# Attention with an exact row maximum: maxima turned and keys loaded earlier, output stores later, the sums copied by VectorE, some maxima sent from two queues

## The chip, the core and the metric

The kernel runs on one core of a Trainium2 chip. Five engines work side by side, each on its own list of instructions in order: TensorE (PE, with its weight loads as PEld), VectorE (DVE), ScalarE (ACT), GpSimd (POOL) and SyncE (SP), which here only issues transfers. They meet through semaphores. A transfer (DMA) is issued by SP, ACT or POOL and then moved by 16 DMA engines. The metric is the device time of one execution in microseconds (us); lower is better. A time is the median of several runs, and one further execution was profiled.

## The reference

One transformer block on 2048 tokens of width 640, all in float32:

```
h  = x + attention(layernorm(x), wqkv) @ wo        # 32 heads of width 20, softmax over 2048 keys
h2 = h + (silu(layernorm(h) @ w_gate) * (layernorm(h) @ w_up)) @ w_down     # inner width 1728
```

The softmax subtracts the maximum of each row of scores, so the kernel needs, for every head and query, the largest of 2048 scores before it can take the exponentials of that row.

## The kernel before

**Stages.** Up to about 319 us the kernel normalizes x and computes queries, keys and values, and also the first maxima. From 319 to 1440 us it does attention. After that come the output projection of the last tokens and the gated two-layer part, whose weights were prepared during attention.

**Units and steps.** Attention is cut into 32 units. Unit u = 4 g + c handles the four heads of group g (8 groups) and the 512 queries of chunk c (4 chunks). A unit has 16 steps, one for each tile of 128 keys (`kt`). What a step does on the engines is set by the string `WhSmsSHMs`, letter by letter:

- `S`, `s` (four in all): scores of 128 keys against 512 queries for one head (line L1328, into one of four PSUM banks named `ps_one`), then the exponential on ACT (L1334, into `probs`).
- `m`, `M`: one 128x512 product for the row maxima of a later unit (L272 into one of three banks named `ps_max`) and its reduction on DVE (L292). `h` and `H`: two half products into one bank and one reduction (L307). So DVE has three reductions in a step.
- `W`: the weighing (L1338) of values by the exponentials of two steps ago, into the bank `acc` of the unit. With the last tile of a unit, which falls into step 1 of the next one, `row_sums` copies `acc` to the SBUF tile `o` on ACT (L1348), and four transfers on SP bring the row sums out of it (L1351, `r<-o`). After `W` come the calls that fell due for this step (`later`) and one task of the weight preparation, which works on POOL and SP (L1146, L1147, L1178 to L1242; stores L1137; loads of raw weights L1166, L1220).

**The maxima of a later unit.** When the last product of unit v has been reduced, `max_all` reduces its partial maxima to a tile `neg` (L315, DVE). This happens in the last step of a unit (v with c = 1), at step 5 (v with c = 2 and c = 0) or step 11 (v with c = 3). The maxima must stand as two extra rows in the queries of v (`q_stk`) before the first score of v. There are two ways.

- With long lead (22 units): `max_parts` splits `neg` in two parts on POOL, `max_turn` transposes them on DVE four steps later (L331) and stores them to DRAM (L332, `m_d<-turned`), and `max_load` reads them into the query rows six steps later (L342, four transfers `q_stk<-m_d`).
- With short lead (10 units: the first two and all with c = 3): `max_finish`, two steps later, transposes on PE (L347, into a `ps_one` bank), splits on ACT (L89) and DVE (L90) into a tile `m2`, and writes the rows with four transfers on SP (L354, `q_stk<-m`).

**The sums of the unit before.** At the end of step 4 DVE takes reciprocals of the row sums (L1359), which waits for `r<-o`; SP stores them (L1361), and reads them back spread over 128 partitions (L1367, `rb<-r_d`), which waits for the store. At the end of step 9 POOL multiplies `o` by them (L1373), and at the end of step 11 SP issues four stores of `o` (L1376). In the last two units all this is earlier.

**Loads.** At the end of step 6 SP loads the queries of unit u + 3 (four transfers). The keys of the next group are loaded in the units with c = 1, at the end of steps 8, 10, 12 and 14 (`load_keys`, four transfers each), the values of the next group in the units with c = 2 at the same steps (one transfer each).

SP works through all of this in one line: an issue that waits for its data holds back every issue written behind it.

Of the kernel before, what the change touches and what calls it, by code (L numbers as in the profile page):

```python
# [13 lines left out]
AF = mybir.ActivationFunctionType  # L14
# [16 lines left out]
NG = H // G  # L31
# [13 lines left out]
def tile_block(ctx: ExitStack, tc: tile.TileContext, x, wqkv, wo, wg, wu, wd, out):  # L45
    nc = tc.nc
# [41 lines left out]
    def split(src, hi, lo, lo_engine=nc.vector):  # L88
        nc.scalar.activation(hi, src, AF.Copy)  # L89
        lo_engine.tensor_tensor(out=lo, in0=src, in1=hi.bitcast(F32), op=ALU.subtract)  # L90
# [221 lines left out]
    def max_all(u):  # L312

        ends[u] = stk.tile([P, G * TPC], F32, name="neg", tag="neg", bufs=2)
        nc.vector.tensor_reduce(  # L315
            ends[u], mxs[u].rearrange("p b h t k -> p (b h t) k"), axis=AX.X, op=ALU.max, negate=True
        )
# [10 lines left out]
    def max_turn(u):  # L328

        turned = stk.tile([P, 2 * G * TPC], F32, name="turned", bufs=2)  # L330
        nc.vector.transpose(turned, ends.pop(u).bitcast(F32).rearrange("p i n -> p (i n)"))  # L331
        nc.sync.dma_start(m_d[u % 2], turned)  # L332

    def max_load(u):

        n = 2 * TPC
        rows = m_d[u % 2].rearrange("(q i r) c -> i r q c", q=4, i=2)
        for b in range(2):
            for i in range(2):
                row = b * ROW + NPART + i  # L340
                dst = queries[u][row : row + 1].bitcast(F32).rearrange("r j c -> r (j c)")
                nc.sync.dma_start(dst, rows[i, b * n : (b + 1) * n])  # L342

    def max_finish(u):

        m = (ps_one if u else ps_max)()[: G * TPC, :P]
        nc.tensor.transpose(m, ends.pop(u), ident)  # L347
        parts = stk.tile([G * TPC, 2, P], F32R, name="m2", tag="m2", bufs=1)
        split(m, parts[:, 0], parts[:, 1], nc.vector)
        for b in range(2):  # L350
            for i in range(2):
                row = b * ROW + NPART + i
                first = b * 2 * TPC
                nc.sync.dma_start(  # L354
                    queries[u][row : row + 1].bitcast(F32).rearrange(
                        "r j (t p) -> r (j t) p", t=TPC
                    ),
                    parts[first : first + 2 * TPC, i, :].bitcast(F32),
                )
# [963 lines left out]
    def scores(u, kt, j, probs):  # L1323

        p, b = divmod(j, 2)
        rows = slice(b * ROW, b * ROW + NPART + 2)
        ps = ps_one()
        nc.tensor.matmul(  # L1328
            ps,
            keys[u // NC][rows, p, kt * P : (kt + 1) * P],  # L1330
            queries[u][rows, p, :],
            start=True, stop=True,
        )
        nc.scalar.activation(probs[p][:, b, :], ps, AF.Exp, scale=scale)  # L1334
# [10 lines left out]

    def row_sums(acc, *queues):
        o = pc.tile([P, CH], F32, name="o", bufs=2)
        nc.scalar.activation(o, acc, AF.Copy)  # L1348
        r = pc.tile([P, 16], F32, name="r")
        for j in range(G):  # L1350
            queues[j % len(queues)].dma_start(  # L1351
                r[32 * j : 32 * j + 32, :],
                o[32 * j + DH : 32 * j + DH + 1, :].rearrange("r (p f) -> r p f", p=32),
            )
        return o, r
# [24 lines left out]
    todo, tail, accs, later, full, now = [], [], {}, {}, [], [0]  # L1380
    left = {u: sum(2 for a in rest if a[0] == u) for u in range(1, NU)}

    whole, halves_of = [], []

    def counted(u, n):
        left[u] -= n
# [3 lines left out]
    def next_max(b):  # L1390
        if not whole and rest:
            a = rest.pop(0)
            whole.extend((*a, i) for i in (b, 1 - b))
        if whole:
            a = whole.pop(0)
            max_one(*a)
            counted(a[0], 1)

    def next_half(b):

        if not halves_of and rest:
            a = rest.pop(0)
            halves_of.extend((i, a, []) for i in range(2))
        if not halves_of:
            return
        i, a, banks = halves_of[0]
        if not banks:
            banks.append(ps_max())
            max_half(banks[0], i, *a, b)
        else:  # L1410
            nc.tensor.keepalive_nop([nc.tensor.lower_ap(banks[0])])
            max_half(banks[0], i, *a, b)
            max_halves(banks[0], i, *a)
            counted(a[0], 2 * i)
            halves_of.pop(0)
# [11 lines left out]
    preparing = prepare_weights()  # L1427
# [3 lines left out]
    for u in range(NU):  # L1431
        g, c = divmod(u, NC)
        if g == NG - 1 and c >= 2:
            _, first, ln, flips, _ = ahead
            extra = [*first, *ln, lambda: None, *flips]
        for kt in range(NT):
            now[0] = u * NT + kt
            probs = [pp.tile([P, 2, CH], F32, name="probs") for _ in range(2)]
            heads = [[0, 2], [1, 3]]
            for op in ORDER if rest or whole or halves_of else LAST_ORDER:  # L1440
                if op in "mM":
                    next_max(int(op == "M"))
                elif op in "hH":
                    next_half(int(op == "H"))
                elif op in "sS":
                    scores(u, kt, heads[op == "S"].pop(0), probs)
                else:
                    if len(todo) == 2:
                        weigh_next()
                    for f in later.pop(now[0], ()):  # L1450
                        f()
                    if extra:
                        extra.pop(0)()
                    if preparing and u and kt not in (3, 4):
                        preparing.pop(0)()
                    if now[0] == (NU - NC) * NT + 8:
                        unit_ring, last_ring = weight_rings()
                        unit_ring.fill()
                        last_ring.fill()
            todo.append((u, kt, probs))  # L1460
            for v in full:
                max_all(v)
                if v % NC == NC - 1 or v == 1:
                    later.setdefault(now[0] + 2, []).append(lambda v=v: max_finish(v))
                else:
                    max_parts(v)
                    later.setdefault(now[0] + 4, []).append(lambda v=v: max_turn(v))
                    later.setdefault(now[0] + 6, []).append(lambda v=v: max_load(v))
            full.clear()
            if kt == 6 and u + 3 < NU:  # L1470
                load_queries(u + 3)
            if kt == 10 and u == 0:
                fill_ones(k_stk[1])
            if kt >= 8 and kt % 2 == 0 and c == 1 and g + 1 < NG:
                load_keys(g + 1, slice((kt - 8) // 2 * CH, (kt - 6) // 2 * CH))
            if kt >= 8 and kt % 2 == 0 and c == 2 and g + 1 < NG:
                load_values(g + 1, (kt - 8) // 2 * TPC, (kt - 6) // 2 * TPC)

            sooner = u >= NU - 2
            if kt == (3 if sooner else 4) and tail:  # L1480
                reciprocals(u - 1, tail[0][2], nc.sync)
                rb = spread(u - 1, nc.sync)
            if kt == (6 if sooner else 9) and tail:
                store_o(u - 1, tail[0][1], rb, nc.gpsimd, None)
            if kt == (7 if sooner else 11) and tail:
                store_o(u - 1, tail.pop()[1], rb, None, nc.sync)
            if g == NG - 1 and c >= 1:
                at = 8 if sooner else NT - 4
                if kt == at:
                    ahead = projection(  # L1490
                        c - 1, ps_max if c < NC - 1 else (lambda: ps_b())
                    )
                if kt in (at, at + 1, 12 if sooner else 14):
                    ahead[0][min(kt - at, 2)]()
                    if kt == at + 1 and c < NC - 1:
                        ahead[4]()
            k = 2 * (u - NU + 8)
            if kt in (12, 13) and 0 <= k + kt - 12 < ND:
                if k + kt == 12:
                    assert not preparing  # L1500
                    wo_hi = pc.tile([P, ND, D], F32R, name="wo_hi", bufs=1)
                    wo_lo = pc.tile([P, ND, D], F32R, name="wo_lo", bufs=1)
                load_wo(k + kt - 12)
            if kt in (2, 3) and 0 <= k + kt - 4 < ND:
                split_wo(k + kt - 4)
# [4 lines left out]
    u, o, r = tail.pop()  # L1510
# [561 lines left out]
```

## Time and profile before

| what | value |
|---|---|
| time, median of 3 runs | 2011.97 us (2009.52 to 2014.36) |
| the profiled execution's own time | 2012.87 us |
| its span, first to last instruction | 2010.4 us |
| granted TensorE clock, mean | 0.999 |
| busy over the span | PE 99%, DVE 80%, ACT 72%, POOL 39% |
| from 319 to 1300 us of the span | 981.00 us: PE 975.77, ACT 965.69, DVE 888.61, POOL 310.81 busy |

A row of the timeline has the start in us from the span's start, the duration in us, the engine, the line, the operation, what it writes and reads, the shapes and a count of equal instructions in a row. In brackets stands how long the engine had been idle before it, and what ended the idle time. `SPq` and `POOLq` mark the issue of a transfer. A row of the transfers' view gives the line, the count, the size of one in KB and the median time from issue to landing, which is known for POOL's issues only. PE's ends are modelled, so its busy share is no measure of its pace; here the distance from one weighing (L1338) to the next is the length of a step.

### The profile page before, as it was taken

How to read it: one execution, taken by the hardware profiler on the slowest of the kernel's cores; microseconds unless marked ns; L12 is line 12 of the kernel's file. 1: busy time of each engine (PE TensorE's matmuls, PEld its weight loads, DVE VectorE, ACT ScalarE, POOL GpSimd, SP SyncE). 2: the span in 40 equal slices, each digit the busy share in tenths (PEclk: the TensorE clock that was granted, in tenths of full speed). 3: DMA queues.
4: the chain of work that ended last, by engine and by line, in shares of the span. 5: the costliest groups of instructions: out<-in, count | busy, mean ns of one | idle time of the engine just before them, and what ended most of it. 6: DMA issues, size and time to landing. Idle time of an engine off the chain costs nothing. (4 is left out here: it accounts for less than half of the span.)

```text
span 2010.4 us, 41923 instructions
## 1 busy us (share of the span) xinstructions
PE 1985.1 (99%) x14794; PEld 1268.7 (63%) x14794; DVE 1599.5 (80%) x2831; ACT 1440.1 (72%) x2827; POOL 789.4 (39%) x1182
## 2 busy tenths in 40 slices
PE   8999999999999999999999999999999999999998
PEld 6999995444444444444444444455598888888887
DVE  5687778899999899998999999975477666676667
ACT  4678778999999999999999999987633222212221
POOL 7464424343453443443400011011155544844465
PEclk9999999999999999999999999999999999999999
DMA  7887563443634544435412132222268655974642
GB/s 244 255 258 257 183 206 78 128 140 105 193 103 141 152 135 138 157 127 175 150 60 68 40 86 58 79 63 62 62 215 278 228 168 174 359 248 160 203 146 93
DMA packets 199350, 310.48 MB, mean 154 GB/s; under 512 B 53744, under 2 KB 87856, under 8 KB 198120
## 3 DMA queue, kind: packets, MB, share of 16 engines
q1 hardware_dynamic: 192552, 284.21, 44.0%
q0 software_dynamic: 6496, 23.60, 4.0%
q8 instruction: 120, 1.97, 0.4%
q14 instruction: 86, 0.70, 0.1%
q10 hardware_dynamic: 96, 0.00, 0.0%
HBM read 208.11 MB, written 99.19 MB: 153 GB/s over the span
## 5 line engine op out<-in xcount | busy, mean ns | idle before, releaser
L1334 ACT ACTIVATE probs<-ps_one 128x512 f32<-128x512 f32 x2048 | 1056.1, 612 | 46.7 <-PE ps_one L1328 37.2
L292 DVE TENSOR_REDUCE mx<-ps_max 128x1 f32<-128x512 f32 x980 | 671.8, 686 | 90.6 <-PE ps_max L272 88.0
L272 PEld LDWEIGHTS ps_max<-k_stk,q_stk 60*128 60x128 f32 x1964 | 294.2, 185 | 462.8 <-DVE mx L307 393.5
L1328 PE MATMUL ps_one<-q_stk,k_stk 62*128 62x512 f32 x2048 | 570.4, 427 | 2.7 <-DMA q_stk<-m 1.8
L272 PE MATMUL ps_max<-k_stk,q_stk 60*128 60x256 f32 (+1 forms) x1964 | 565.5, 376 | 2.5 <-DVE mx L292 1.2
L1338 PE MATMUL acc<-probs,v_stk 128*32 128x512 f32 x4096 | 546.1, 605 | 0.1
L307 DVE TENSOR_REDUCE mx<-ps_max 128x2 f32<-128x512 f32 x492 | 335.8, 683 | 0.4 <-PE ps_max L272 0.4
L1328 PEld LDWEIGHTS ps_one<-q_stk,k_stk 62*128 62x128 f32 x2048 | 304.9, 184 | 15.0 <-ACT probs L1334 11.3
L1750 DVE TENSOR_TENSOR tmp<-ps_a,tmp 128x512 f32<-128x512 f32 x208 | 141.3, 690 | 122.2 <-PE ps_a L1535 96.6
L262 DVE TENSOR_REDUCE mx<-ps_max 128x2 f32<-128x512 f32 x288 | 180.8, 685 | 63.7 <-PE ps_max L240 60.2
L252 ACT ACTIVATE ps_max<-ps_max 128x512 f32<-128x512 f32 x288 | 151.6, 583 | 42.9 <-PE ps_max L240 40.3
L1629 PE MATMUL ps_b<-halves,yp 128*128 128x320 f32 x1032 | 179.0, 308 | 1.5 <-DMA halves<-j_d 1.3
L1629 PEld LDWEIGHTS ps_b<-halves,yp 128*128 128x128 f32 x1032 | 165.2, 188 | 17.5 <-POOL yp L90 1.5
L1535 PE MATMUL ps_a<-t,units 128*128 128x512 f32 x624 | 162.5, 396 | 0.0
L1338 PEld LDWEIGHTS acc<-probs,v_stk 128*32 128x32 f32 x4096 | 80.7, 108 | 128.1 <-issue 119.9
L90 POOL TENSOR_TENSOR yp<-y,yp 128x256 fp32r<-128x256 f32 x96 | 60.2, 628 | 189.7 <-ACT yp L89 189.7
L1535 PE MATMUL ps_a<-z,units 128*128 128x512 f32 x516 | 133.8, 394 | 0.0
L1535 PEld LDWEIGHTS ps_a<-t,units 128*128 128x128 f32 x624 | 112.6, 188 | 18.5
L1373 POOL TENSOR_TENSOR o<-o,rb 128x512 f32<-128x512 f32 x31 | 39.8, 1284 | 194.2 <-DMA rb<-r_d 60.6
L1634 DVE TENSOR_TENSOR h<-ps_b,h 128x320 f32<-128x320 f32 x248 | 110.1, 482 | 6.8 <-PE ps_b L1629 5.4
L671 PE MATMUL ps_one<-z_hi,w_lo 64*128 64x512 f32 x380 | 113.4, 392 | 0.0
L671 PE MATMUL ps_one<-z_lo,w_hi 64*128 64x512 f32 x380 | 112.1, 392 | 0.0
(228 smaller groups left out, 2746.5 us busy)
## 6 DMA issues: line engine op xcount, KB each, us to landing
units<-w_d SPq DMA_DIRECT2D x186, 256.0 KB
w_d<-stage SPq DMA_DIRECT2D x106, 256.0 KB
halves<-j_d SPq DMA_DIRECT2D x70, 320.0 KB
j_d<-stage SPq DMA_DIRECT2D x42, 320.0 KB
k_stk<-k_d SPq DMA_DIRECT2D x64, 160.0 KB
q_stk<-q_d SPq DMA_DIRECT2D x64, 160.0 KB
raw<-k_d SPq DMA_DIRECT2D x62, 160.0 KB
raw<-q_d SPq DMA_DIRECT2D x54, 160.0 KB
```

The costliest lines, as they stand in the source:

```text
L252: nc.scalar.activation(ps, ps, AF.Relu)
L262: nc.vector.tensor_reduce(mx[:, b, :, t, kc], ps.rearrange("p (j n) -> p j n", j=2), axis=AX.X, op=ALU.max,)
L272: nc.tensor.matmul(ps, queries[u][rows, pair, t * P : (t + 1) * P], keys[u // NC][rows, pair, k0:k1], start=True, stop=True, skip_group_ch ...
L292: nc.vector.tensor_reduce(mx[:, b, pair, t, kc : kc + 1], ps, axis=AX.X, op=ALU.max)
L307: nc.vector.tensor_reduce(max_slots(u)[:, :, pair, t, slot], ps.rearrange("p (j n) -> p j n", j=2), axis=AX.X, op=ALU.max,)
L671: nc.tensor.matmul(ps, a[rows], b[rows], start=(i == n == 0), stop=(i == 1 and n == last), skip_group_check=True,)
L1328: nc.tensor.matmul(ps, keys[u // NC][rows, p, kt * P : (kt + 1) * P], queries[u][rows, p, :], start=True, stop=True,)
L1334: nc.scalar.activation(probs[p][:, b, :], ps, AF.Exp, scale=scale)
L1338: nc.tensor.matmul(acc[32 * j : 32 * j + 32, :], values[u // NC][:, kt, j * VW : j * VW + 32], probs[j // 2][:, j % 2, :], start=(kt == 0) ...
L1535: nc.tensor.matmul(ps.rearrange("p (t n) -> p t n", t=TPC), w[k][:, i], z[k][:, :, j], start=(first and m == 0), stop=(last and m == len(n ...
L1629: nc.tensor.matmul(ps, a, b, start=(n == 0), stop=(n == len(pairs) - 1))
L1750: add = lambda out, ps, x: nc.vector.tensor_tensor(out=out, in0=ps, in1=x, op=ALU.add)
```

## The change

- `max_finish` is called at the end of the step behind the one in which `max_all` stood, that is ahead of the `W` which it used to follow. In the step in which it is due, the task of weight preparation is left out and comes one later. Its two transfers for the second half of the rows are issued by POOL, the first two by SP as before.
- `max_turn` comes three steps behind `max_all` instead of four, `max_load` five instead of six.
- The keys of the next group are loaded in units with c = 0 (in the first group still c = 1).
- Reciprocals, their store and `rb` come at the end of step 5 instead of 4; the stores of `o` in units with c = 2 at the end of step 13 instead of 11 (the last two units keep their own steps).
- `row_sums` copies `acc` on DVE instead of ACT, also after the last unit.

```diff
-                nc.sync.dma_start(
+                (nc.gpsimd if b else nc.sync).dma_start(
                     queries[u][row : row + 1].bitcast(F32).rearrange(
...
     def row_sums(acc, *queues):
         o = pc.tile([P, CH], F32, name="o", bufs=2)
-        nc.scalar.activation(o, acc, AF.Copy)
+        nc.vector.tensor_copy(o, acc)
...
-                    if preparing and u and kt not in (3, 4):
+                    if preparing and u and kt not in (3, 4) and not behind_step:
                         preparing.pop(0)()
...
             todo.append((u, kt, probs))
+            while behind_step:
+                behind_step.pop(0)()
             for v in full:
                 max_all(v)
                 if v % NC == NC - 1 or v == 1:
-                    later.setdefault(now[0] + 2, []).append(lambda v=v: max_finish(v))
+                    behind_step.append(lambda v=v: max_finish(v))
                 else:
                     max_parts(v)
-                    later.setdefault(now[0] + 4, []).append(lambda v=v: max_turn(v))
-                    later.setdefault(now[0] + 6, []).append(lambda v=v: max_load(v))
+                    later.setdefault(now[0] + 3, []).append(lambda v=v: max_turn(v))
+                    later.setdefault(now[0] + 5, []).append(lambda v=v: max_load(v))
...
-            if kt >= 8 and kt % 2 == 0 and c == 1 and g + 1 < NG:
+            if kt >= 8 and kt % 2 == 0 and c == (0 if g else 1) and g + 1 < NG:
                 load_keys(g + 1, slice((kt - 8) // 2 * CH, (kt - 6) // 2 * CH))
...
-            if kt == (3 if sooner else 4) and tail:
+            if kt == (3 if sooner else 5) and tail:
                 reciprocals(u - 1, tail[0][2], nc.sync)
...
-            if kt == (7 if sooner else 11) and tail:
+            if kt == (7 if sooner else 13 if c == 2 else 11) and tail:
                 store_o(u - 1, tail.pop()[1], rb, None, nc.sync)
```

On PE, in unit 6, the transposition of `max_finish` for unit 7 stands behind the weighing of step 13 before the change:

```order
L272 MATMUL ps_max<-k_stk_125,q_stk 128x512
L1328 MATMUL ps_one<-q_stk,k_stk_5605 128x512
L1338 MATMUL acc<-probs,v_stk_5606 32x512 x4
L347 MATMUL ps_one<-ident,neg 16x128
L272 MATMUL ps_max<-k_stk_125,q_stk 128x256
```

and now ahead of it:

```order
L272 MATMUL ps_max<-k_stk_125,q_stk 128x512
L1328 MATMUL ps_one<-q_stk,k_stk_5605 128x512
L347 MATMUL ps_one<-ident,neg 16x128
L1338 MATMUL acc<-probs,v_stk_5606 32x512 x4
L272 MATMUL ps_max<-k_stk_125,q_stk 128x256
```

The one weighing and the one transposition have changed places; the scores and products around them stand as before.

On SP, in unit 9 (c = 1), from the store of the turned maxima of unit 10 to the stores of `o`, before:

```order
L332 DMA m_d_70<-turned 128x32
L176 DMA k_stk_5605<-k_d_64 40x2x512
L176 DMA k_stk_5605<-k_d_64 20x2x512
L176 DMA k_stk_5605<-k_d_64 40x2x512
L176 DMA k_stk_5605<-k_d_64 20x2x512
L342 DMA q_stk<-m_d_70 1x32x32 x4
L1376 DMA o_d<-o 20x512 x4
```

and now:

```order
L332 DMA m_d_70<-turned 128x32
L1137 DMA w_d_84<-stage 128x512 x2
L1166 DMA raw<-in_B_w_gate 128x5x128
L1166 DMA raw<-in_B_w_up 128x5x128
L342 DMA q_stk<-m_d_70 1x32x32 x4
L1376 DMA o_d<-o 20x512 x4
```

The key loads have left this unit, and the weight preparation stands a little later in the program than before, so that a load of raw weights now lies between.

On SP, in unit 10 (c = 2), around the rows of maxima for unit 11, before:

```order
L193 DMA v_stk_5606<-v_d 128x4x96 x2
L1376 DMA o_d<-o 20x512 x4
L1137 DMA w_d_86<-stage 128x512
L193 DMA v_stk_5606<-v_d 128x4x96
L354 DMA q_stk<-m_11431 1x8x128 x4
```

and now, where the other two transfers `q_stk<-m` are on POOL:

```order
L193 DMA v_stk_5606<-v_d 128x4x96 x2
L354 DMA q_stk<-m_11412 1x8x128 x2
L193 DMA v_stk_5606<-v_d 128x4x96
L1376 DMA o_d<-o 20x512 x4
L193 DMA v_stk_5606<-v_d 128x4x96
```

The stores of `o`, which wait for POOL's multiplication, have moved behind the rows of maxima.

On POOL the two transfers come directly behind the first sums of the weight preparation (L1178, L1179):

```order
L1373 TENSOR_TENSOR o<-o,rb 128x512
L1178 TENSOR_TENSOR sums<-raw 128x256
L1179 TENSOR_TENSOR sums<-sums,raw 128x256
L354 DMA q_stk<-m_11412 1x8x128 x2
L1182 TENSOR_TENSOR sums<-raw 128x256
```

The two transfers stand between those sums and the next ones. Before, in the same unit, POOL issued none of them and the multiplication stood behind the first sums:

```order
L1178 TENSOR_TENSOR sums<-raw 128x256
L1179 TENSOR_TENSOR sums<-sums,raw 128x256
L1373 TENSOR_TENSOR o<-o,rb 128x512
L1182 TENSOR_TENSOR sums<-raw 128x256
```

So the multiplication has moved ahead of the first sums.

On DVE, in unit 5, the copy of `o` now stands between the last reduction of one step and the first of the next:

```order
L307 TENSOR_REDUCE mx_7742<-ps_max 128x2
L292 TENSOR_REDUCE mx_7742<-ps_max 128x1
L1348 COPY o<-acc 128x512
L292 TENSOR_REDUCE mx_7742<-ps_max 128x1
L307 TENSOR_REDUCE mx_7742<-ps_max 128x2
```

The copy came over from ACT; the reductions around it stand as before.

Later in the same unit the reciprocal follows `max_all` directly:

```order
L307 TENSOR_REDUCE mx_7742<-ps_max 128x2
L292 TENSOR_REDUCE mx_8453<-ps_max 128x1
L315 TENSOR_REDUCE neg<-mx_7742 128x16
L1359 RECIPROCAL r<-r 128x16
L292 TENSOR_REDUCE mx_8453<-ps_max 128x1
```

Before, the reciprocal stood three reductions ahead of `neg`.

More of the change, by code (lines that the diff above doesn't have):

```diff
@@ L1381, in tile_block @@
     left = {u: sum(2 for a in rest if a[0] == u) for u in range(1, NU)}
-    whole, halves_of = [], []
+    whole, halves_of, behind_step = [], [], []
     def counted(u, n):
```

## The prediction

> **What bounds the kernel now.** I read the page for the shares first, then the windows for the attention stage, which holds every edited line but one.
>
> ```profile
> 319.00:1300.00 981.00, 975.77 (x7417) 415.29 (x7414) 888.61 (x1493) 965.69 (x1889) 310.81 (x526) 1.00 0.39 116
> ```
>
> The columns are the stretch, its length, the busy times of PE, PEld, DVE, ACT and POOL, the granted clock and the DMA share. PE and ACT are both almost full, DVE has 92 us left, POOL 670. So work taken off ACT can count, and work put on DVE need not be free. Next, the timeline of a few steps in unit 5.
>
> ```profile
> 491.29 1.06 PE L1338 MATMUL acc<-probs,v_stk 128*32 128x512 f32 x8
> ...
> 493.04 0.39 PE L272 MATMUL ps_max<-k_stk,q_stk 60*128 60x512 f32 x1
> ...
> 493.37 1.07 PE L1338 MATMUL acc<-probs,v_stk 128*32 128x512 f32 x8
> ...
> 495.75 1.07 PE L1338 MATMUL acc<-probs,v_stk 128*32 128x512 f32 x8
> ```
>
> A usual step lasts 493.37 − 491.29 = 2.08; the step that holds ACT's copy of `acc` lasts 2.38. I take 2.07 for a step and .31 for the copy on ACT. The same stretch on DVE:
>
> ```profile
> 492.08 0.68 DVE L292 TENSOR_REDUCE mx<-ps_max 128x1 f32<-128x512 f32 x1
> ...
> 492.94 0.69 DVE L292 TENSOR_REDUCE mx<-ps_max 128x1 f32<-128x512 f32 x1 [0.17 <-PE ps_max L272]
> ...
> 494.14 0.68 DVE L292 TENSOR_REDUCE mx<-ps_max 128x1 f32<-128x512 f32 x1
> ```
>
> From `M`'s reduction at 492.08 to the next at 494.14 are 2.06 with three reductions; reductions without a wait follow each other by .60 (492.94 to 494.14 are two), so .26 are free in each step, and the row with the wait shows that PE ends that slot, not DVE.
>
> Then the places of the copy, one per unit, give the units' lengths.
>
> ```profile
> 391.00 0.63 ACT L1348 ACTIVATE o<-acc 128x512 f32<-128x512 f32 x1
> 425.82 0.63 ACT L1348 ACTIVATE o<-acc 128x512 f32<-128x512 f32 x1
> 526.14 0.63 ACT L1348 ACTIVATE o<-acc 128x512 f32<-128x512 f32 x1
> 559.94 0.63 ACT L1348 ACTIVATE o<-acc 128x512 f32<-128x512 f32 x1
> 593.41 0.60 ACT L1348 ACTIVATE o<-acc 128x512 f32<-128x512 f32 x1
> 626.78 0.63 ACT L1348 ACTIVATE o<-acc 128x512 f32<-128x512 f32 x1
> 660.67 0.63 ACT L1348 ACTIVATE o<-acc 128x512 f32<-128x512 f32 x1
> 697.38 0.63 ACT L1348 ACTIVATE o<-acc 128x512 f32<-128x512 f32 x1
> 797.70 0.63 ACT L1348 ACTIVATE o<-acc 128x512 f32<-128x512 f32 x1
> 832.07 0.63 ACT L1348 ACTIVATE o<-acc 128x512 f32<-128x512 f32 x1
> 898.93 0.63 ACT L1348 ACTIVATE o<-acc 128x512 f32<-128x512 f32 x1
> 933.42 0.63 ACT L1348 ACTIVATE o<-acc 128x512 f32<-128x512 f32 x1
> 968.18 0.63 ACT L1348 ACTIVATE o<-acc 128x512 f32<-128x512 f32 x1
> ```
>
> Units 7 and 8 last 33.47 and 33.37, mean 33.42; unit 6 (c = 2, with a `max_finish`) 33.80. Against these, six units are too long: unit 2 by 34.82 − 33.80 = 1.02, unit 9 by .47, unit 10 by 2.91, unit 14 by .57, unit 17 by 1.07, unit 18 by .96. The sum is 7.00. Unit 10 shows their causes.
>
> ```profile
> 670.89 0.25 DVE L1359 RECIPROCAL r<-r 128x16 f32<-128x16 f32 x1 [1.55 <-DMA r<-o]
> 671.06 0.63 DVE L292 TENSOR_REDUCE mx<-ps_max 128x1 f32<-128x512 f32 x1
> ...
> 671.74 0.38 PE L272 MATMUL ps_max<-k_stk,q_stk 60*128 60x256 f32 x1 [0.74 <-DVE mx L292]
> ```
>
> The reciprocal held DVE for 1.55, and PE could begin its next maxima product .05 after the reduction behind it had ended (671.69): a product waits until a reduction of the step before has freed its bank. The second stall of that unit:
>
> ```profile
> 684.58 0.73 POOL L1178 TENSOR_TENSOR sums<-raw 128x256 f32<-128x256 f32 x1 [20.96 <-DMA raw<-in_B_w_up]
> ...
> 686.09 1.28 POOL L1373 TENSOR_TENSOR o<-o,rb 128x512 f32<-128x512 f32 x1
> ...
> 687.39 1.42 SPq L1376 DMA_DIRECT2D o_d<-o  x4
> ...
> 690.85 2.82 SPq L354 DMA_DIRECT2D q_stk<-m  x4
> ...
> 694.96 0.47 PE L1328 MATMUL ps_one<-q_stk,k_stk 62*128 62x512 f32 x1 [1.20 <-DMA q_stk<-m]
> ```
>
> POOL waited for raw weights, so its multiplication was late, so SP's stores of `o` were late, and the maxima queued behind them came when PE had stood for 1.20. In unit 9 the key loads ahead on SP did the same to `q_stk<-m_d`:
>
> ```profile
> 653.99 2.79 SPq L342 DMA_DIRECT2D q_stk<-m_d  x4
> ```
>
> **The change part by part.** *The copy.* One of the same shape stands on DVE earlier in the program:
>
> ```profile
> 318.94 0.69 DVE L758 COPY e<-ps_one 128x512 f32<-128x512 f32 x1 [0.67 <-issue]
> 319.54 1.28 DVE L262 TENSOR_REDUCE mx<-ps_max 128x2 f32<-128x512 f32 x2
> ```
>
> It takes .60 of DVE before the next can start. In the step's .26 slot it fits by that much, and DVE falls back by .34 to .35. PE notices at `M`: its bank is free when the reduction ends at 492.08 + .68 = 492.76, and its product came at 493.04, so it has .28 − .05 = .23 to spare. PE loses .35 − .23 = .12, once, since the following slots give DVE .26 each back. Per unit −.31 + .12 = −.19, for 29 units −5.5. Bounds: the copy is hidden (−.31 × 29 = −9.0), or nothing absorbs the .35 and the new reader also frees `acc` .06 later than ACT did (+.10 × 29 = +2.9). I take −5.5, because both rows used are of the same step kind. After the last unit the copy stands alone:
>
> ```profile
> 1444.39 0.60 ACT L1348 ACTIVATE o<-acc 128x512 f32<-128x512 f32 x1 [0.95 <-PE acc L1338]
> ```
>
> .69 for .60: +.1.
>
> The Trainium skill ("VectorE: DVE Perf Modes", section "The DRAIN you can't avoid") says that the next VectorE operation does not start until the pipeline of the one before has emptied. By that the copy would take its full .69, DVE would fall back by .43, PE by .20, the copy would gain .11 × 29 = 3.2, and the sum below would be −10.1, 2002.8. The trace disagrees: the .69 copy at 318.94 is followed .60 later, and so are the .68 reductions.
>
> *Reciprocals one step later.* They come 2.07 later, more than the 1.08 of unit 2's stall or the 1.55 of unit 10's. In units with c = 1 or 3 they now follow `neg` directly and delay DVE by about .2, which the .23 covers: 0, at most .2 × 15 = 3 if it is not. The store of the reciprocals and `rb` also come a step later on SP, still four steps ahead of the multiplication that waits for them.
>
> *Keys in c = 0.* Sixteen transfers leave SP's line in c = 1, where `q_stk<-m_d` waited behind them, and join it in c = 0, where at steps 8 to 14 nothing that is due soon stands behind them: the row sums of the next unit are issued in step 1 and needed at step 5. First group unchanged. Price 0; its gain is the stalls of units 9 and 17. Bound: a like stall moves into c = 0, .47 to 1.07 for each of six units, at most +6.4.
>
> *Stores of `o` in c = 2 at step 13.* Two steps later on SP; the rows of maxima (end of step 12) pass them, so POOL's lateness ends at a store that nobody waits for. The tile `o` has a second buffer. This removes the second stall of units 10, 14 and 18.
>
> *Turn and load a step sooner.* DVE's transpose and four issues are the same in number; `max_turn` waits for POOL's split, now with three steps' lead, 6.2 us. Price 0.
>
> Together the six stalls go: −7.0. Bounds: half of them stays (−3.5); none does.
>
> *`max_finish` ahead of `W`.* In unit 6:
>
> ```profile
> 549.91 1.06 PE L1338 MATMUL acc<-probs,v_stk 128*32 128x512 f32 x8
> 550.91 0.28 PE L347 MATMUL ps_one<-ident,neg 128*16 128x128 f32 x1
> 551.11 0.38 PE L272 MATMUL ps_max<-k_stk,q_stk 60*128 60x256 f32 x1
> ...
> 551.59 0.28 DVE L90 TENSOR_TENSOR m<-ps_one,m 16x128 fp32r<-16x128 f32 x1 [0.21 <-ACT m L89]
> ...
> 557.48 0.50 PE L1328 MATMUL ps_one<-q_stk,k_stk 62*128 62x512 f32 x1
> ```
>
> The transposition takes .20 of PE (550.91 to 551.11) on either side of `W`, and ACT reaches its part only behind the exponentials of the step, wherever it stands. So 0. It needs a bank of the scores, and may wait for one sooner: bounds −.2 (it fills a wait) to +.4 (it waits and the next score waits after it) in each of seven units, −1.4 to +2.8. The preparation task left out comes a step later; POOL has the room.
>
> *Two transfers by POOL.* The maxima are ready at 551.59 + .28 = 551.87, unit 7's first score comes at 557.48: 5.6 us. The nearest rows for POOL's issues, with the median from issue to landing last:
>
> ```profile
> q_d<-e POOLq DMA_DIRECT2D x7, 64.0 KB, 4.1
> ...
> k_d<-e POOLq DMA_DIRECT2D x2, 64.0 KB, 6.4
> ```
>
> The second issue comes some .7 behind the first (2.82 for four on SP). At 4.1 it lands after 4.8, in time: 0. At 6.4 it lands after 7.1, 1.5 late, in each of the eight units before one with c = 3: +12. I take 4.1, because these have 8x128 floats, 4 KB, and the lighter row is nearer.
>
> Sum: −5.5 + .1 − 7.0 = −12.4. The profiled execution took 2012.87, .9 over the median and within its spread: 2012.87 − 12.4 = **2000.5**.
>
> **The rivals.** *The copy is hidden wholly*: −9.0 + .1 − 7.0 = −15.9, 1997.0. For it: the .35 is spread over steps. Against it: the .23 from the rows above. *The copy is not absorbed*: 2.9 in place of −5.5, 2008.9. For it: DVE is at 91%. *Stalls move instead of going*: raw loads now stand ahead of `q_stk<-m_d` on SP, and can wait for POOL; half of 7.0 remains (2004.0) or up to 6.4 comes anew (2006.9). Against it: in c = 0 the next row on SP that is due soon comes in step 1 of the next unit.
>
> *GpSimd's half of the maxima is late.* Now PE waits for a second queue, and those issues stand in POOL's line behind sums that wait for raw weights (20.96 idle at 684.58). At 6.4 it eats the gain: −12.4 + 12 = −.4, 2012.5. The decision lies at a landing of 7.0, counted from m ready and without the .7: (7.0 + .7 − 5.6) × 8 = 16.8, less 12.4, is +4.4. At 7.5, 6.4 and a wait of 1.1 behind a multiplication (1.28), it is 20.8 − 12.4 = +8.4, **2021**. Against it: in the rows of unit 10 the raw weights were there 3 us before the maxima, and of POOL's 981 us only 311 are busy.
>
> The Trainium skill ("SBUF — State Buffer", section "SBUF: two separate sides") warns that GpSimd cannot write the descriptors of its transfers while VectorE runs a two-port copy. With DVE at 91% that would give the late case. No run here shows POOL's issues during attention, and the new copy reads PSUM, so I leave the chance where the rows put it.
>
> **How the numbers follow.** Forecast .50; copy hidden .06; not absorbed .08; stalls moved .10; GpSimd late up to the gain .12; later .14. Some 4 us (0.2%) are what a measurement here can tell from no change. Faster: the first four, .74; same .12; slower .14. The range goes from 1996.5 to 2010.5, which holds the first four and a part of the fifth, .8.
>
> **What would show it.** Steps with the copy near 2.2 and no `<-ACT o` in PE's waits; no idle DVE ahead of L1359 above .3; units 2, 10, 14, 17 and 18 within .3 of the others of their c; the first score of units with c = 3 not waiting for `q_stk<-m`. Wrong would be: idle PE at those first scores (POOL's landing), idle DVE at L331 or L1359, or copy steps at 2.38 as before.

## The result

| | median | runs |
|---|---|---|
| before | 2012.36 us | 8, 2009.52 to 2014.36 |
| after | 2003.92 us | 8, 2001.27 to 2008.49 |

The ratio is 0.9962, with a 95% interval of 0.9953 to 0.9971: 8.4 us gained where 12.4 had been forecast. The profiled execution of the changed kernel is the slowest of its eight (2008.49), so its trace is read place by place and not by its sum.

The windows of the changed kernel over the same stretch of attention, with the columns as before:

```profile
319.00:1300.00 981.00, 977.74 (x7459) 410.26 (x7462) 906.68 (x1529) 962.65 (x1871) 320.10 (x543) 1.00 0.39 116
```

DVE went from 888.61 to 906.68 busy, and ACT from 965.69 to 962.65, though more of the work lies in these 981 us now (ACT's copies are gone, exponentials have come in).

The start of unit 12, first the timeline of PE and then that of DVE:

```profile
728.07 1.07 PE L1338 MATMUL acc<-probs,v_stk 128*32 128x512 f32 x8
...
730.19 1.07 PE L1338 MATMUL acc<-probs,v_stk 128*32 128x512 f32 x8
...
732.42 0.64 PE L1338 MATMUL acc<-probs,v_stk 128*32 128x512 f32 x4
```

```profile
728.86 0.68 DVE L292 TENSOR_REDUCE mx<-ps_max 128x1 f32<-128x512 f32 x1
729.46 0.68 DVE L1348 COPY o<-acc 128x512 f32<-128x512 f32 x1
730.05 0.68 DVE L292 TENSOR_REDUCE mx<-ps_max 128x1 f32<-128x512 f32 x1
...
731.25 0.68 DVE L292 TENSOR_REDUCE mx<-ps_max 128x1 f32<-128x512 f32 x1
```

The copy holds DVE for .59 (729.46 to 730.05). PE pays twice for it. The weighing at 730.19 begins .05 after the copy ends (729.46 + .68 = 730.14), so its step lasts 2.12: the bank `acc` comes free too late. The next step lasts 2.23, because the reduction at 731.25 ends at 731.93 and the last maxima product of that step, which needs its bank, starts only .06 later:

```profile
731.99 0.50 PE L272 MATMUL ps_max<-k_stk,q_stk 60*128 60x512 f32 x1
```

In unit 8 of this execution stands a wait that no unit had before (DVE, PE and POOL in three fences):

```profile
596.78 0.21 DVE L331 STREAM_TRANSPOSE turned<-neg 128x32 f32<-128x32 f32 x1 [1.98 <-POOL neg L324]
```

```profile
597.62 0.38 PE L272 MATMUL ps_max<-k_stk,q_stk 60*128 60x256 f32 x1 [1.28 <-DVE mx L292]
```

```profile
593.37 0.73 POOL L1178 TENSOR_TENSOR sums<-raw 128x256 f32<-128x256 f32 x1 [12.74 <-DMA raw<-in_B_w_up]
...
596.24 0.20 POOL L323 CAST neg<-neg 128x16 fp32r<-128x16 f32 x1
596.53 0.22 POOL L324 TENSOR_TENSOR neg<-neg,neg 128x16 fp32r<-128x16 f32 x1
```

POOL waited 12.74 us for raw weights. The split of the maxima, which `max_turn` needs, stood behind the four sums that follow, and DVE reached the transposition, now a step sooner, before POOL had split. DVE's reductions behind it stood, and PE after them. Unit 8 lasts 36.61 instead of 33.43.

Not all of these 3.2 us are the wait. Right behind it the granted clock is down for 3.4 us, as the windows of this profile show in the last column but two:

```profile
598.60:602.00 3.40, 3.40 (x18) 1.08 (x15) 2.05 (x4) 1.74 (x4) 3.16 (x8) 0.50 0.45 163
```

Four later profiles with the copy on DVE have a wait of .23 to .90 at the same place and a clock of 1.00 there. In them unit 8 is longer by DVE's wait, or by up to .1 less. By that the wait of 1.98 costs some 1.9 (an estimate), and the lost clock the other 1.3. The last section comes back to this loss.

GpSimd's half of the maxima was never late. The transfers' view after:

```profile
q_stk<-m POOLq DMA_DIRECT2D x20, 4.0 KB, 1.8
```

The lengths of some units, from the first score of one to the first score of the next, worked out from the traces of five kernels of which the last three are explained below:

```
unit  before  before again  after  after again  finish back
  2    34.82     33.95      34.65     33.84        34.08
  4    33.39     33.47      33.37     33.35        33.36
  8    33.43     33.51      36.61     34.17        33.38
  9    33.92     33.70      33.41     33.41        33.42
 10    36.72     35.32      33.74     33.74        34.98
 14    34.39     34.43      33.74     33.75        33.72
 17    34.52     34.48      33.49     33.42        33.42
 18    34.76     34.91      33.74     33.74        35.23
 30    53.67     53.65      54.15     54.13        53.64
```

Five of the six long units (9, 10, 14, 17, 18) are short after the change; unit 2 is still long in the first profile and short in the second. Unit 8 is new, and unit 30 is .5 longer.

In unit 2 of the first profile DVE waits at the reciprocal as it did before the change (1.03, before 1.07), though the reciprocal comes a step later now. SP's issues are shown behind DVE's row:

```profile
401.95 0.25 DVE L1359 RECIPROCAL r<-r 128x16 f32<-128x16 f32 x1 [1.03 <-DMA r<-o]
```

```profile
393.64 0.43 SPq L1166 DMA_DIRECT2D raw<-in_B_w_gate  x1
394.12 0.60 SPq L1166 DMA_DIRECT2D raw<-in_B_w_up  x1
394.82 3.90 SPq L1351 DMA_DIRECT2D r<-o  x4
```

The first row of sums is issued 3.84 us behind the end of the copy, where it was 1.91 before the change. So SP was later by about as much as the reciprocal.

### The profile page after: what moved, and what is told of

Same layout as the page of the kernel before. It is cut to its first block, busy times and chain, and to the rows that moved or that the text cites. A ratio compares the mean times of both kernels' runs of the same rounds, so it can differ in the third digit from the quotient of the medians.

```text
span 2006.7 us, 41862 instructions
## 1 busy us (share of the span) xinstructions
PE 1981.1 (99%) x14794; PEld 1260.7 (63%) x14794; DVE 1616.4 (81%) x2863; ACT 1430.1 (71%) x2795; POOL 800.7 (40%) x1202
## 5 line engine op out<-in xcount | busy, mean ns | idle before, releaser
L1328 PE MATMUL ps_one<-q_stk,k_stk 62*128 62x512 f32 x2048 | 564.5, 425 | 0.9 <-DVE m L90 0.9
L90 POOL TENSOR_TENSOR yp<-y,yp 128x256 fp32r<-128x256 f32 x96 | 60.3, 628 | 189.7 <-ACT yp L89 189.7
```

What stands on the lines that cost most here:

```text
L1328: nc.tensor.matmul(ps, keys[u // NC][rows, p, kt * P : (kt + 1) * P], queries[u][rows, p, :], start=True, stop=True,)
```

## The experiments

Each comparison is made on one chip; the medians of before were 2014.09, 2014.26 and 2011.83 beside the first, second and third group of four.

**The changed kernel again, and the kernel before again.** No edit.

> The changed kernel once more, for a second profile. If the 1.98 us wait of DVE for GpSimd's split in unit 8 belongs to the order of the work, it stands at the same place again and the median stays near 2004. If it comes from when raw weights happen to land, unit 8 lasts 33.4 as its neighbours and the profiled span is some 3 us shorter, or the wait stands in another unit. A usual step of 2.07 (2.068 before, 2.074 in the first profile) would say that the longer step belonged to that execution alone.

> The kernel before, for a profile on the chip of the runs around it. Its usual step was 2.068 in the profile before and 2.075 in all profiles of the edited kernels. If the step belongs to the chip or the day, it is 2.075 here too; if the copy on VectorE made it longer, 2.068. Long units: 10 above all, and units 2, 9, 14, 17, 18, by sums between 5 and 9 us.

Measured for the changed kernel: 2008.13 beside 2014.09, ratio 0.9967 (0.9955 to 0.9979), a gain of 6.0 where the first comparison had 8.4. Unit 8's wait stands at the same place, and is .90 instead of 1.98, as the timeline of DVE shows:

```profile
603.98 0.21 DVE L331 STREAM_TRANSPOSE turned<-neg 128x32 f32<-128x32 f32 x1 [0.90 <-POOL neg L324]
```

PE's timeline in unit 30 of that profile has the other new wait:

```profile
1385.24 0.50 PE L1328 MATMUL ps_one<-q_stk,k_stk 62*128 62x512 f32 x1 [0.92 <-DVE m L90]
```

In the slower steps of the last units, a score now waits for the subtraction of `max_finish` (L90) to free its bank.

The kernel before: one execution, 2013.57. Its six long units are too long by 4.3 in sum, less than the 5 to 9 expected. Its usual step is 2.075, the same as in the profiles after on that chip. So the 2.068 of the profile before was a matter of the execution, not of the kernel: a later profile of an edited kernel shows 2.068 again. At equal steps the first three steps of a quiet unit, the ones around the copy, last 6.522 before and 6.411 after (means over twelve units without other waits, in both pairs of profiles alike to .01). The copy's move is worth .11 a unit.

**The copy alone, and all but the copy.** The first kernel puts the copy on ACT in the changed kernel, the second puts it on DVE in the kernel before:

```diff
-        nc.vector.tensor_copy(o, acc)
+        nc.scalar.activation(o, acc, AF.Copy)
```

```diff
-        nc.scalar.activation(o, acc, AF.Copy)
+        nc.vector.tensor_copy(o, acc)
```

> The changed kernel with the copy of acc on ScalarE as before. My prediction's price (.19 a unit) gives 5.5 us more than the changed kernel, 2009.5. What the profile after shows (step 1 lasts 2.12, step 2 2.23: .21 lost to DVE against .31 on ACT) gives .10 x 29 = 3 us more, 2007. If the copy costs the same on both engines, the same 2004.

> The kernel before with only the copy of acc on VectorE. By the prediction 5.5 us under before (2006.9), by the profile after 3 us under (2009.4), and if it costs the same on both, no difference. The six long units (2, 9, 10, 14, 17, 18) stay long, since SP's order is unchanged.

Measured: 2009.11 with ACT's copy in the changed kernel, 1.0 over it, whose interval (0.9957 to 0.9979) overlaps the changed kernel's; and 2012.04 with the copy alone, 2.0 under before, ratio 0.9994 (0.9985 to 1.0002). The time alone does not settle it. The profiles do: the three steps last 6.525 with ACT's copy and 6.403 with DVE's. So the copy is worth .11 to .12 in each of 29 units, 3.3 us, and neither 5.5 nor nothing. With the copy alone the long units stay (9, 10 and 18 last 35.15, 35.77 and 36.63).

**The old leads.** `max_turn` four steps and `max_load` six behind `max_all`:

```diff
-                    later.setdefault(now[0] + 3, []).append(lambda v=v: max_turn(v))
-                    later.setdefault(now[0] + 5, []).append(lambda v=v: max_load(v))
+                    later.setdefault(now[0] + 4, []).append(lambda v=v: max_turn(v))
+                    later.setdefault(now[0] + 6, []).append(lambda v=v: max_load(v))
```

> The changed kernel with max_turn four and max_load six steps behind max_all, as before. If the shorter lead is what let the wait of unit 8 in, no DVE wait at L331 in the profile, and a median lower by 0 to 3 us (2001 to 2004) with a smaller spread. The rival, that an earlier q_stk<-m_d is needed now, gives PE waits for q_stk<-m_d at the first step of units and 1 to 3 us more.

Measured: 2004.88 (2003.61 to 2005.84, 5 runs), ratio 0.9953 (0.994 to 0.9965), where the changed kernel beside it had 2008.13 (2005.26 to 2014.26). The timeline of DVE in unit 8:

```profile
596.04 0.20 DVE L331 STREAM_TRANSPOSE turned<-neg 128x32 f32<-128x32 f32 x1
```

The wait is gone, and no other took its place: unit 8 lasts 33.36. How much of the 3.2 us between the medians belongs to the lead is not shown: the two ratios' intervals overlap, the changed kernel's profile of this group loses only .8 in unit 8, and two kernels below that have the short lead gain nearly as much over before (ratios 0.9961 and 0.9963). That the wait belongs to the lead rests on the profiles. In eight profiles of kernels with a lead of three steps (the changed kernel's two and six variants'), DVE waited in unit 8 for 1.98, 1.33, .90, .74, .43, .23 and twice not at all; in six with a lead of four steps, the kernel before among them, never. How late POOL is varies from one execution to the next with the landing of the raw weights.

**Keys in c = 1.**

```diff
-            if kt >= 8 and kt % 2 == 0 and c == (0 if g else 1) and g + 1 < NG:
+            if kt >= 8 and kt % 2 == 0 and c == 1 and g + 1 < NG:
```

> The changed kernel with the keys of the next group in units with c = 1 again. If the key loads on SP are what delayed q_stk<-m_d, units 9 and 17 are long again by .5 to 1.7 at their last step, and the median is 1.5 to 3 us over the changed kernel's. The reciprocals are a step later, so unit 10's first wait stays away. The rival (a turn one step earlier suffices for the load) gives no difference.

Measured: 2007.26 beside 2014.26, ratio 0.9963 (0.9949 to 0.9976), which is the changed kernel's own. Units 9 and 17 last 33.41 both, as the rival had it. The keys' place alone was not what shortened them.

**Keys in c = 1 and the old leads together.** Both edits from above.

> The changed kernel with both the keys in c = 1 and the leads of four and six steps of before. Either one alone left units 9 and 17 at 33.41. If they covered for each other, as my account of SP's line has it, units 9 and 17 are long again by .5 to 1.3 and the median is 2 to 3 us above the kernel with the old leads alone (2004.9). If the left-out preparation task cured them, nothing moves.

Measured: 2006.64 beside 2011.83, ratio 0.9978 (0.9969 to 0.9987). Unit 9 lasts 34.91, and unit 13, which had been short, 34.47; unit 17, which was to be long too, lasts 33.38. SP, and PE at the first score of unit 10:

```profile
649.81 1.96 SPq L176 DMA_DIRECT2D k_stk<-k_d  x4
651.81 3.08 SPq L342 DMA_DIRECT2D q_stk<-m_d  x4
```

```profile
657.58 0.47 PE L1328 MATMUL ps_one<-q_stk,k_stk 62*128 62x512 f32 x1 [1.19 <-DMA q_stk<-m_d]
```

The key loads ahead on SP make the rows of maxima late, as the prediction had it. Either the keys' move or the sooner load is enough against it in unit 9: the two cover the same stall. The gain over before is 5.2, against 9.2 with the old leads alone, and the two ratios' intervals do not overlap. What shortened unit 17 is not shown.

**The stores of `o` at step 11 everywhere.**

```diff
-            if kt == (7 if sooner else 13 if c == 2 else 11) and tail:
+            if kt == (7 if sooner else 11) and tail:
```

> The changed kernel with all stores of o at step 11, ahead of the rows of maxima on SP. If POOL's late multiplication reaches the maxima through SP's line, units 10, 14 and 18 are long again at their last step, by 1.6, .6 and .9 as before, 3 us in all. If sending half by GpSimd was what cured it, or the key loads, none of them is long and the time does not move.

Measured: 2006.04 beside 2014.26, ratio 0.9964 (0.9951 to 0.9976). Units 10, 14 and 18 last 33.74 each, so the stores' place is not what shortened them. The timeline of POOL in unit 10 shows why, and that of SP behind it:

```profile
678.97 1.28 POOL L1373 TENSOR_TENSOR o<-o,rb 128x512 f32<-128x512 f32 x1 [13.27 <-DMA rb<-r_d]
684.88 0.74 POOL L1178 TENSOR_TENSOR sums<-raw 128x256 f32<-128x256 f32 x1 [4.63 <-DMA raw<-in_B_w_up]
...
686.37 1.03 POOL L354 DMA_DIRECT2D q_stk<-m  x2
```

```profile
682.16 1.95 SPq L1376 DMA_DIRECT2D o_d<-o  x4
684.96 1.47 SPq L354 DMA_DIRECT2D q_stk<-m  x2
```

The multiplication now stands ahead of POOL's wait for raw weights instead of behind it, so `o` is there in time wherever its store stands.

**`max_finish` behind `W`, with no task left out.**

```diff
-                    behind_step.append(lambda v=v: max_finish(v))
+                    later.setdefault(now[0] + 2, []).append(lambda v=v: max_finish(v))
```

> The changed kernel with max_finish behind W, and no preparation task left out. Units with c = 2 last 33.74 after and 33.80 before, the others 33.37 and 33.42, so the place costs the same either way: no difference within 1 us. Unit 30, which is .5 longer after the change, tells whether that belongs to this edit (53.6 again) or to another (54.1).

Measured: 2008.00 beside 2014.26, ratio 0.9968 (0.9958 to 0.9978); 2.0 over the stores' kernel and .7 over the keys' kernel of the same group. Units 10 and 18 are long again by 1.2 and 1.5, and unit 30 has its 53.64 back. Unit 10 on POOL, SP and PE:

```profile
683.36 0.74 POOL L1178 TENSOR_TENSOR sums<-raw 128x256 f32<-128x256 f32 x1 [17.55 <-DMA raw<-in_B_w_up]
...
684.86 1.27 POOL L1373 TENSOR_TENSOR o<-o,rb 128x512 f32<-128x512 f32 x1
...
689.78 1.03 POOL L354 DMA_DIRECT2D q_stk<-m  x2
```

```profile
688.71 0.34 SPq L1137 DMA_DIRECT2D w_d<-stage  x1
...
689.62 1.48 SPq L354 DMA_DIRECT2D q_stk<-m  x2
```

```profile
692.91 0.47 PE L1328 MATMUL ps_one<-q_stk,k_stk 62*128 62x512 f32 x1 [0.86 <-DMA q_stk<-m]
```

Here the raw weights' wait stands ahead of the multiplication again, and the tasks of preparation run into both queues: POOL issues its half after eight of their instructions, and SP's half stands behind a store `w_d<-stage` that waits for POOL. So the edit that I had priced at nothing is the only one that brings these two stalls back when it alone is undone. Which half of it does so, the earlier place or the task left out, stays open; the order of POOL's work differs by the task. Unit 14 stays short here (33.72), and what shortened it is not shown.

**Reciprocals at step 4.**

```diff
-            if kt == (3 if sooner else 5) and tail:
+            if kt == (3 if sooner else 4) and tail:
```

> The changed kernel with reciprocals, their store and rb at step 4. My prediction had the later place remove the first wait of units 2 and 10 (1.0 and 1.3 to 1.6). If so, a DVE wait at L1359 in unit 2 or 10 and up to 2.5 us more than the changed kernel. If earlier key loads already bring r<-o in time in unit 10, only unit 2 is long, by up to 1. In units of odd number the .2 of the reciprocal behind neg goes away: some .0 to .1 for each of 15 if it ever cost anything.

Measured: 2002.71 beside 2011.83, ratio 0.9961 (0.9949 to 0.9974). No wait at L1359; units 2 and 10 last 33.81 and 33.71. With the rest of the change in place the later step was not needed in this profile. In the kernel with the copy alone, which has everything else of before, DVE waited there for .41, .89 and 1.55 in units 2, 10 and 18. In units 10 and 18 two parts of the change cover the wait. With the keys in c = 0, SP issues the first `r<-o` .03 us behind the end of the copy in this profile (unit 10, where it was 3.58 before), so the reciprocals can stay at step 4. With the keys in c = 1 and the reciprocals at step 5, it comes 3.73 behind the copy in unit 18, and the reciprocal, 9.88 behind the copy, still waits for nothing. Ahead of unit 2 stands unit 1, the only unit with c = 1 that still loads keys. There the later step does not always suffice: besides the 1.03 of the first profile, DVE waits for .18 and .47 in the profiles with the keys in c = 1 and with `max_finish` behind `W`. In the odd units up to 27 the reciprocal behind `neg` cost at most some .15: they last 33.35 to 33.40 here and 33.37 to 33.50 in the changed kernel's second profile.

**All four transfers by SP.**

```diff
-                (nc.gpsimd if b else nc.sync).dma_start(
+                nc.sync.dma_start(
```

> The changed kernel with all four transfers of max_finish on SP. In the traces GpSimd's half lands 1.6 to 4.2 us after its issue and 1 us or more before the first score that needs it, and SP alone took 2.8 us for the four and 1.3 more to land. If neither queue is ever last, no difference within 1.5 us and the first scores of units with c = 3 wait for nothing. If the second queue is what keeps units 10, 14 and 18 short, they wait for q_stk<-m again, 1 to 3 us in all.

Measured: 2002.98 beside 2011.83, ratio 0.9963 (0.995 to 0.9977): no difference, and no first score waits.

**The copy cut in two.** With the old leads, and

```diff
-        nc.vector.tensor_copy(o, acc)
+        nc.vector.tensor_copy(o[:, :352], acc[:, :352])
+        nc.scalar.activation(o[:, 352:], acc[:, 352:], AF.Copy)
```

> The changed kernel with the old leads (four and six steps), and with the copy of acc cut in two: VectorE takes 352 columns, ScalarE 160. By my working of VectorE's slot, 352 columns hold it for some .43, so it falls back by .17, under the .23 that M has to spare, and PE loses nothing to it; ScalarE's part is an estimate of .22 from .48 for 512 columns, of which its slack of .16 in a step takes most. Steps 0 to 2 together 6.25 to 6.33 instead of 6.41, 2 to 5 us under the kernel with the old leads (2004.9): 2000 to 2003. If the wait is for acc to come free and not for VectorE's time, the three steps stay at 6.41 or rise.

Measured: 2013.57 beside 2011.83, ratio 1.0007 (0.9998 to 1.0016): the copy's gain is gone and more. The three steps last 6.80. DVE, ACT and PE at the start of unit 12:

```profile
728.86 0.51 DVE L1348 COPY o<-acc 128x352 f32<-128x352 f32 x1
729.29 0.68 DVE L292 TENSOR_REDUCE mx<-ps_max 128x1 f32<-128x512 f32 x1
```

```profile
729.46 0.30 ACT L1349 ACTIVATE o<-acc 128x160 f32<-128x160 f32 x1 [0.46 <-POOL stage L1146]
```

```profile
729.81 0.64 PE L1338 MATMUL acc<-probs,v_stk 128*32 128x512 f32 x4 [0.21 <-ACT o L1349]
```

DVE's part is as short as I had worked out (.43 from start to start). ACT's part did not run beside it: ACT stood for .46 and began .09 after DVE's part had ended (729.37), and the next weighing waited for ACT. The view names a POOL row as what ended ACT's wait, but in all 32 units ACT's part begins .03 to .09 after DVE's has ended, and both write the same tile. Whether the chip or the program's own dependencies order the two parts was not settled.

## Why the prediction was right, and where it was off

- **The sign and the range hold**: 2003.92 is inside 1996.5 to 2010.5, and faster by 8.4 where 12.4 was forecast. That the size came so near is in part luck, since several causes below were named wrongly. Two of the prediction's own signs of being wrong were there in the first profile: idle DVE at L331 (1.98, unit 8) and at L1359 (1.03, unit 2).
- **The copy was sized too well.** The step of the prediction that failed is "PE loses .12, once", with the release of `acc` .06 later kept only for the upper bound. Both terms are paid, one after the other: .05 in the step of the copy and .16 in the next. The gain is .11 a unit and 3.3 us, not 5.5. The row by which the copy takes .60 of DVE held (.59).
- **The rule of the Trainium skill on the pipeline's drain** ("VectorE: DVE Perf Modes", section "The DRAIN you can't avoid") would have given .11 a unit, which is what was measured, but by another way: DVE's next operation came .59 after the copy's start, not .68. The agreement of the sums is chance. The same section says that a next operation which is not held starts earlier, which the prediction left out; the .59 agrees with that.
- **Five of the six long units became short, but not by the causes named.** The wait for `r<-o` in unit 10 had two remedies, the keys' move and the later step; in unit 2 it was still there in the first profile, against "more than the 1.08 of unit 2's stall". The late `q_stk<-m_d` of unit 9 was due to key loads, as forecast, and either of two edits cures it; for unit 17 the remedy stays open. The late `q_stk<-m` of units 10, 14 and 18 was put down to the stores of `o` on SP; putting these back changed nothing, while putting `max_finish` back with its task made units 10 and 18 long again; for unit 14 the remedy stays open. The step that failed is "This removes the second stall of units 10, 14 and 18". Also, 7.00 was the sum of one execution: the kernel before had 4.3 in its second profile, with the units' lengths at that chip's step taken as 33.50 and 33.87.
- **The shorter lead was priced at 0 and costs.** "`max_turn` waits for POOL's split, now with three steps' lead" named the dependence, but took POOL to be free, though the row of POOL's 20.96 us wait stood in the same prediction. The wait costs 0 to some 1.9 in an execution.
- **`max_finish` ahead of `W`** costs nothing in the usual units (33.74 after, 33.80 and 33.87 before) and .5 in unit 30, where steps are of another kind.
- **The account.** 12.4, less 2.2 for the copy, .5 for unit 30 and, by execution, 0 to 1.9 for unit 8 and 0 to .9 for unit 2, leaves 6.9 to 9.7 of gain; if the kernel before stalls for 4.3 instead of 7.0, it is 2.7 less. Measured were 8.4 and, on the chip of the second profile, 6.0.
- **GpSimd's half late**, the rival on the slower side, did not come: 4 KB landed in 1.8 us at the median, and in the latest case of the first profile (4.1 us) still 1.0 ahead of the first score. The Trainium skill's warning ("SBUF — State Buffer", section "SBUF: two separate sides") is about VectorE's two-port operations, for which it names copies from SBUF to SBUF, and this copy reads PSUM. With DVE at 92% (906.68 of 981) no landing came too late here; what stretched some from 1.6 to 4.2 us stays open.

## What to carry to other kernels

When work moves to an engine with a slot free in each period, price every resource it holds apart: its time on the engine and the buffer that it frees, since here both were paid one after the other. A queue that can wait long for a transfer, as POOL does for raw weights, makes everything behind it late in some executions and not in others; before shortening a lead, ask what stands ahead of the producer on its engine. And where several edits aim at the same stall, undo them in pairs: each alone looked useless, both together brought the stall back.

## What was not expected of the hardware

The same kernel had a usual step of 2.068 in one execution and 2.075 in another, .3%, at a mean granted clock of 0.999 both times; over the 464 steps of units 0 to 28 that is 3 us, as much as the copy.

All fourteen profiles also show a loss of granted clock for some 3.4 us during attention. In thirteen of them it falls in unit 0, as in the windows of the profile before:

```profile
323.00:325.00 2.00, 1.94 (x10) 0.23 (x8) 1.58 (x3) 1.59 (x4) 2.00 (x1) 0.55 1.00 254
```

The clock is .55 here in the last column but two. Unit 0 lasted 36.16 in that execution and 36.0 to 36.2 in the other twelve, but 34.65 in the first profile of the changed kernel, where the same steps show a clock of 1.00. There the loss stands in unit 8 instead, behind the wait (.50 from 598.60 to 602.00, above). So the 1.5 us that unit 0 is shorter in that execution are no gain: most of them come back in unit 8. Three profiles (keys in c = 1, alone and with the old leads, and the copy cut in two) have a second such loss, in unit 30, which lasts 55.3 to 55.4 there instead of 54.1; the first of them shows it in these windows:

```profile
1376.00:1378.00 2.00, 2.00 (x12) 0.86 (x5) 0.00 (x0) 0.84 (x2) 0.00 (x0) 0.50 0.00 0
```

What sets the loss off, and whether the wait of unit 8 did so, is not shown. A unit's length should be read beside the granted clock of the same stretch before its excess is put down to an edit.
